# Moving a third query chunk's attention forward, parking its sums in DRAM, and cutting the last chunk and the K/V projections into halves

## The chip, the core and the metric

The kernel runs on one core of one Trainium2 chip. The metric is the device time of one execution in microseconds (us), as the median of several executions. Most executions of one kernel agree within 0.3%. Where two kernels are compared, the ratio is the mean time of one kernel's fast runs over that of the other's of the same rounds, so it is not quite the ratio of the medians quoted beside it. Chips and sessions differ a little (the kernel before took 2823 us in one session and 2825 to 2830 in the others), so experiments are compared by their ratio to the kernel before, measured on the same chip in the same call. A point is 1% of the time of the kernel before.

## The reference

Two kinds of layer alternate, A B A B, on `x` of shape 1 x 2048 x 1024, with 32 heads of 32:

```python
def A(x, wqkv, w_phi, wo):            # linear attention with feature maps
    q, k, v = split(x @ wqkv)
    pq, pk = q @ w_phi, k @ w_phi                       # per head, 32 x 32
    phi = lambda p: concat(softmax(p), softmax(-p))     # over 32 features
    kv = phi(pk).T @ v;  z = phi(pk).sum(rows)
    return (phi(pq) @ kv / (phi(pq) @ z + 1e-6)) @ wo
def B(x, wqkv, wo):                   # softmax attention
    q, k, v = split(x @ wqkv)
    return softmax(q @ k.T * 32**-0.5) @ v @ wo
x = x + A(layernorm(x)); x = x + B(layernorm(x))
x = x + A(layernorm(x)); x = x + B(layernorm(x))
```

The kernel has two passes of the same shape. I call them layer 1 and layer 2; each is the query side of an A layer followed by a B layer. Layer 1 also computes, after its B attention, the key side of the next A layer. That extra work makes the end of layer 1 heavier than the end of layer 2.

## The kernel before

The sequence is cut into four chunks of 512 rows (C), each of four key tiles of 128. A *step* of attention handles two key tiles, 256 queries (a half) and four heads (a head group; there are 8). It makes 8 score matmuls, two exps on ScalarE of 128 x 1024, and 16 matmuls into one accumulator `ND` in PSUM, whose left half is the numerator and whose right half is the denominator:

```python
    LAYOUT = {"wide": (0, 8), "mid": (2, 3), "narrow": (3, 1)}   # score tiles, background PSUM slots
    ...
    def step(self, q, kv, g, half, kc, begin, end, ...):   # 8 matmuls, then 2 exps
    def finish(self):                                      # one step later: 16 matmuls into ND
        ...
        if not end:
            return
        num, den = nd[:, 0:QH], nd[:, QH:C]
        if not last:                       # this query will see more keys later
            a = acc[0][g // 2][:, g % 2, half, :]          # numerator stays in SBUF
            if half == 0:
                self.dt = T("dt", [P, 2, QH], F32)         # ONE buffer
            ...
            DVE.tensor_tensor(out=a, in0=num, in1=a, op=ALU.add)
            DVE.tensor_tensor(out=dt[:, half, :], in0=den, in1=dn[:, half, :], op=ALU.add)
            if half == 1:                                  # denominator goes to DRAM
                for j in range(4):
                    SP.dma_start(out=den_d[acc[1]][g:g + 1, j, :, :], in_=dt[32 * j:32 * j + 1, :, :])
            return
        ...                                # else: add, reciprocal, multiply into oT
```

All other work (projections, layer norms, output projections) is *background*: Python generators, pumped between steps. A credit per step (`per`, in units of 512 columns of TensorE work) sets how much. `bg.until(name)` runs the rest of a generator with no attention between: a *flush*.

```python
            bg = Background(); set_mode("mid")
            bg.add("b0", b_proj(0, (1,)))
            bg.add("b1", rest1())                     # chunk 1: rest of A, K, V, Q
            attend(att, att.block(qs[0], 0, 4, ...), bg, 10)
            bg.until("b1")                            # flush
            set_mode("narrow")
            bg.add("b2", to_b(2)); bg.add("b3", to_b(3))
            attend(att, att.block(qs[0], 4, 8, ...), bg, 5)
            attend(att, att.block(qs[1], 0, 8, ...), bg, 5)
            bg.until("b2")
            attend(att, att.block(qs[0], 8, 12, ...), bg, 6)
            attend(att, att.block(qs[1], 8, 12, ...), bg, 6)
            bg.until("b3")                            # flush
            for i in range(NCH):
                ...                                   # after(i-1): output projection, and in layer 1
                                                      # the next A layer's key side ("follow-up")
                block = (att.block(qs[i], 0, 16, ...) if i > 1
                         else att.block(qs[i], 12, 16, ...))
                attend(att, block, bg, 3.5)
            settle(att); bg.until("after2")
            set_mode("wide")
            drain(after(3, oT[-1], layer, True))      # the tail: no attention left
```

PE, ScalarE, VectorE and Pool instructions keep the order in which this Python code emits them.

The softmax here doesn't subtract the row's maximum and nothing guards it: scores larger than these inputs give would overflow.

Of the kernel before, what the change touches and what calls it, by code (L numbers as in the profile page):

```python
# [32 lines left out]
def kernel(  # L33
# [14 lines left out]
    def ppf(w):  # L48
# [7 lines left out]
        w=3, c8=3, x=2, q=2, kv=2, st=2, E=6, ea=8, acc=4, f=5, r=3, nd=2,  # L56
# [29 lines left out]
    den_d = [Dr(f"den_d{i}", [G, 4, 2, QH], F32) for i in range(2)]  # L86
# [87 lines left out]
    def mm8(ps, lhsT, rhs):  # L174
        for po in range(G):
            mm(ps, lhsT(po), rhs(po), po == 0, po == G - 1)
            if po == 3:
                yield 4, False
# [3 lines left out]
    def ln_gen(x, res, fast=False):  # L182
        ps = ps512()
        yield from mm8(ps, lambda po: ones_bf[:], lambda po: x[:, po, :])
        m = T("f", [P, C], F32)
        DVE.tensor_scalar(out=m[:], in0=ps, scalar1=1.0 / D, scalar2=None, op0=ALU.mult)
        yield 4, True
        xc = T("c8", [P, G, C], BF16)
        res["xc"] = xc
        sqs = []  # L190

        def centre(po):
            DVE.tensor_tensor(out=xc[:, po, :], in0=x[:, po, :], in1=m[:], op=ALU.subtract)  # L193

        ps = ps512()
        for po in range(G):
            centre(po)
            if po % 4 == 0:
                sq4 = T("st", [P, 4, C], BF16)
            sq = sq4[:, po % 4, :]  # L200
            if fast:
                SC.activation(out=sq, in_=xc[:, po, :], func=ACT.Square)
            else:
                DVE.tensor_tensor(  # L204
                    out=sq, in0=xc[:, po, :], in1=xc[:, po, :], op=ALU.mult
                )
            sqs.append(sq)
        yield from wait(3)
        for po in range(G):
            mm(ps, ones_bf[:], sqs[po], po == 0, po == G - 1)  # L210
            if po < G - 1 and po % 2:
                yield 2, False
        lnv = T("f", [P, C], F32)
        rstd = T("r", [P, C], F32)
        SC.activation(out=lnv[:], in_=ps, func=ACT.Ln, scale=1.0 / D, bias=eps_t[:])
        SC.activation(out=rstd[:], in_=lnv[:], func=ACT.Exp, scale=-0.5)
        yield 2, True

        diag = T("f", [P, 4, P], F32)
        rcol = T("rcol", [P, 4], F32)  # L220
        DVE.tensor_tensor(
            out=diag[:], in0=rstd[:].rearrange("p (t q) -> p t q", q=P),
            in1=ident[:].unsqueeze(1).to_broadcast([P, 4, P]), op=ALU.mult,
        )
        DVE.reduce_sum(out=rcol[:], in_=diag[:], axis=AX.X)
        if fast:
            ncol = T("nc", [P, 4], F32)
# [21 lines left out]
    def ak_gen(c, x, get, fast=False, res=None, hook=None):  # L249
        if c == 0:  # L250
# [6 lines left out]
        SP.dma_start(out=xa_d[c][:], in_=xc[:])  # L257
        SP.dma_start(out=ra_d[c][:], in_=rstd[:])
        va = []
        for i in range(2):  # L260
            v = T(f"acc{2 + 2 * (c % 2) + i}", [P, 2, G, P + 1], BF16)
            POOL.memset(v[:, :, :, P:P + 1], 1.0)
            va.append(v)
        for fc in range(2):
            w = get()
            for t in range(4):
# [12 lines left out]
        for fc in range(2):  # L279
            w = get()  # L280
            es = []
            for t in range(4):
# [33 lines left out]
            def kv_part(fc=fc, es=es):  # L316
                for gi in range(4):
                    g = fc * 4 + gi
                    ps = ps512()
                    for t in range(4):  # L320
                        for s in range(2):
# [4 lines left out]
                                t == 0 and s == 0, t == 3,  # L326
                            )
                    if c == 0:
# [6 lines left out]
                    yield 2.5, True  # L335
# [114 lines left out]
    def aq_gen(c, x, slabs, res, pause=6):  # L450
# [9 lines left out]
    def aq_finish(c, x, slabs, res):  # L460
        yield from proj_out(x, res["oT"], slabs)
        yield from ln_gen(x, res, PS["ns"] == 0)
        SP.dma_start(out=x_d[c][:], in_=x[:])

    def proj_out(x, oT, slabs):
        for ft in range(G):
            if ft % 4 == 0:
                w = slabs.get()
            ps = ps512()
# [4 lines left out]
            yield 4, True  # L474


    def bkv_gen(c, res, slabs, h, q=None):
# [24 lines left out]
        if q is not None:  # L502
            yield from bq_gen(q, xc, rstd, slabs, range(4 * h, 4 * h + 4))
# [13 lines left out]
    class Attention:  # L517
# [4 lines left out]
        def load(self, k0, k1, g, acc, first):  # L522
# [7 lines left out]
            if first:  # L530
                return kt, None
            dn = T("dn", [P, 2, QH], F32)
            for j in range(4):
                SP.dma_start(  # L534
                    out=dn[32 * j:32 * j + 32, :, :],
                    in_=den_d[acc[1]][g:g + 1, j, :, :].to_broadcast([DH, 2, QH]),
                )
            return kt, dn

        def block(self, q, k0, k1, acc, oT, first, last, before=None):  # L540

            kv = self.load(k0, k1, 0, acc, first)
            for g in range(G):
                if before and g in before:
                    before[g]()
                    kv = self.load(k0, k1, g, acc, first)
                nxt = None
                for half in range(2):
                    for kc in range(0, k1 - k0, 2):
                        self.step(q, kv, g, half, kc, kc == 0, kc + 2 == k1 - k0,  # L550
                                  acc, oT, first, last)
                        if nxt is None and g + 1 < G and not (before and g + 1 in before):
                            nxt = self.load(k0, k1, g + 1, acc, first)
# [3 lines left out]
        def step(self, q, kv, g, half, kc, begin, end, acc, oT, first, last):  # L557
# [23 lines left out]
            self.lag.append((kv, dn, g, half, kc, begin, end, acc, oT, first, last, es))  # L581

        def finish(self):

            kv, dn, g, half, kc, begin, end, acc, oT, first, last, es = self.lag.pop(0)
# [18 lines left out]
            if not last:  # L604
                a = acc[0][g // 2][:, g % 2, half, :]
                if half == 0:
                    self.dt = T("dt", [P, 2, QH], F32)
                dt = self.dt
                if first:
# [7 lines left out]
                if half == 1:  # L617
                    for j in range(4):
                        SP.dma_start(
                            out=den_d[acc[1]][g:g + 1, j, :, :], in_=dt[32 * j:32 * j + 1, :, :]  # L620
                        )
                return
            ndc = T("nd", [P, C], F32)
            if first:
                DVE.tensor_copy(out=ndc[:], in_=nd[:])  # L625
            else:
                DVE.tensor_tensor(
                    out=ndc[:, 0:QH], in0=num, in1=acc[0][g // 2][:, g % 2, half, :], op=ALU.add
                )
                DVE.tensor_tensor(out=ndc[:, QH:C], in0=den, in1=dn[:, half, :], op=ALU.add)  # L630
            rc = T("rc", [P, QH], F32)
            DVE.reciprocal(out=rc[:], in_=ndc[:, QH:C])  # L632
            DVE.tensor_tensor(
                out=oT[:, g, half * QH:(half + 1) * QH], in0=ndc[:, 0:QH], in1=rc[:],
# [75 lines left out]
    def run():  # L710
# [19 lines left out]
        drain(ln_gen(xs[0], res, True))  # L730
        for c in range(NCH):
# [12 lines left out]
            main = ak_gen(c, xs[c], iter(av + pk).__next__, True, res, hook)  # L744
            if c + 1 < NCH:
                xs[c + 1] = load_first(c + 1)
                drain(merge(main, ln_gen(xs[c + 1], nres, True), 4))
# [5 lines left out]
        def after(c, oT, layer, fast=False):  # L753
            x = load_x(c)
            sl = Slabs(["bo"] + (["av", "pk"] if layer == 0 else []))
            sl.prefetch()
            yield from proj_out(x, oT, sl)
            if layer == 0:
                yield from ak_gen(c, x, sl.get, fast)
                SP.dma_start(out=x_d[c][:], in_=x[:])  # L760
            else:
                yield from store_out(c, x)
# [8 lines left out]
        for layer in range(2):  # L771
# [4 lines left out]
            BKVQ = ["bk0", "bv0", "bq0", "bk1", "bv1", "bq1"]  # L776

            def to_b(c):
                x = load_x(c)
                res = saved[c] = {}  # L780
                sl = res["sl"] = Slabs(["pq", "ao"] + BKV)
                yield from aq_gen(c, x, sl, res)
                yield from b_proj(c, (0, 1))
                SP.dma_start(out=xb_d[c][:], in_=res["xc"][:])
                SP.dma_start(out=rb_d[c][:], in_=res["rstd"][:])

            def b_proj(c, parts):
                res = saved[c]
                for h in parts:
                    yield from bkv_gen(c, res, res["sl"], h, qs.get(c))  # L790
# [5 lines left out]
            r0["sl"] = Slabs(["ao"] + BKVQ)  # L796
            r1["sl"] = Slabs(["ao"] + BKVQ)
# [5 lines left out]
            early = [T(f"acc{4 + k}", [P, 2, 2, C], BF16) for k in range(4)]  # L803
            es1 = [early[g // 2][:, g % 2] for g in range(G)]
# [12 lines left out]
            drain(b_proj(0, (0,)))  # L817

            def rest1():
# [3 lines left out]
                yield from b_proj(1, (0, 1))  # L823

            bg = Background()
            set_mode("mid")
            bg.add("b0", b_proj(0, (1,)))
            bg.add("b1", rest1())
            acc = [([T(f"acc{k}", [P, 2, 2, QH], F32) for k in range(4)], 0), None]
            attend(  # L830
                att,
                att.block(qs[0], 0, 4, acc[0], None, True, False, {4: lambda: bg.until("b0")}),
                bg, 10,
            )
            settle(att)
            bg.until("b1")
            acc[1] = ([T(f"acc{4 + k}", [P, 2, 2, QH], F32) for k in range(4)], 1)
            set_mode("narrow")
            bg.add("b2", to_b(2))
            bg.add("b3", to_b(3))  # L840
            attend(att, att.block(qs[0], 4, 8, acc[0], None, False, False), bg, 5)
            attend(att, att.block(qs[1], 0, 8, acc[1], None, True, False), bg, 5)
            bg.until("b2")
            attend(att, att.block(qs[0], 8, 12, acc[0], None, False, False), bg, 6)
            attend(att, att.block(qs[1], 8, 12, acc[1], None, False, False), bg, 6)
            bg.until("b3")
            oT = [None] * NCH
            for i in range(NCH):
                if 0 < i < NCH - 1:
                    qs[i + 1] = T("q", [P, G, C], BF16)  # L850
                    bg.add(f"q{i + 1}", next_q(i + 1, qs[i + 1]))
                if i:
                    bg.add(f"after{i - 1}", chain(wait(3), after(i - 1, oT[i - 1], layer)))
                bg.until(f"q{i}")
                oT[i] = T("c8", [P, G, C], BF16)
                block = (
                    att.block(qs[i], 0, S // P, None, oT[i], True, True) if i > 1
                    else att.block(qs[i], 12, 16, acc[i], oT[i], False, True)
                )
                attend(att, block, bg, 3.5)  # L860
            settle(att)
            bg.until(f"after{NCH - 2}")
            set_mode("wide")
            drain(after(NCH - 1, oT[-1], layer, True))
# [99 lines left out]
    def store_out(c, x):  # L964
        for t in range(4):
# [42 lines left out]
```

## Time and profile before

Median 2822.97 us of three runs (2821.79 to 2825.78). The top of the profile's page gives busy time and share of the span:

```profile
span 2830.9 us, 89391 instructions
PE 2375.8 (84%) x40048; PEld 1151.2 (41%) x40048; DVE 1326.5 (47%) x2205; ACT 2156.5 (76%) x2489; POOL 95.7 (3%) x87
```

No engine is the limit throughout, so the page's shares say little and the stages say more. Where ScalarE is saturated, an exp starts every 0.91 us (median), so a step costs 1.83 us and the 512 steps of a layer cost about 935 us at the least. The table gives busy time by stretch (from:to, length, then busy time of PE, weight loads, VectorE, ScalarE and Pool with counts, granted clock, DMA share and GB/s). The rows are: all of layer 1 from its first exp to layer 2's first; all of layer 2 to the end; the two flushes of layer 1; the third and the fourth query's attention in layer 1; layer 1's tail; layer 2's tail.

```profile
282.60:1658.10 1375.50, 1152.15 (x20740) 561.38 (x20736) 664.74 (x1030) 1054.96 (x1206) 47.66 (x40) 0.93 0.35 111
1658.10:2830.90 1172.80, 975.22 (x17848) 466.50 (x17843) 472.83 (x819) 970.60 (x1062) 0.00 (x0) 0.95 0.30 97
369.60:412.50 42.90, 42.10 (x796) 20.06 (x792) 17.83 (x26) 0.04 (x1) 0.00 (x0) 1.00 0.62 189
786.60:805.10 18.50, 13.57 (x240) 6.58 (x236) 4.73 (x7) 0.03 (x2) 0.00 (x0) 1.00 0.47 148
941.40:1229.00 287.60, 240.46 (x5024) 124.57 (x5023) 134.07 (x185) 254.02 (x289) 19.18 (x15) 0.95 0.32 104
1229.00:1495.50 266.50, 216.56 (x4322) 107.25 (x4315) 104.16 (x138) 247.87 (x279) 16.45 (x15) 0.96 0.21 70
1495.50:1658.10 162.60, 143.87 (x730) 63.85 (x733) 97.34 (x153) 53.52 (x90) 11.69 (x8) 0.92 0.41 136
2803.50:2830.90 27.40, 21.33 (x110) 10.12 (x109) 12.73 (x43) 0.00 (x0) 0.00 (x0) 0.81 0.10 39
```

Read ScalarE's column against the length. In the flushes it is 0.04 of 42.9 and 0.03 of 18.5: TensorE projects and nobody does exps. In the third query's attention it is 254 of 288; the rest is lost to waits.

From the list of waits (engine, tile and line <- what it waited for: total us, times, longest us), the lines about denominators. `dt` is the tile that is stored to DRAM (`den_d`), `dn` the one loaded back; in later lists `S` is a score tile, `E` its exps and `BG` a background tile in PSUM:

```profile
PE ND L594 <- DVE dt L614: 98.8, 48, 10.2
DVE dt L614 <- DMA den_d<-dt: 44.7, 30, 3.8
DVE nd L630 <- DMA dn<-den_d: 25.1, 22, 4.9
DVE dt L614 <- DMA dn<-den_d: 11.7, 7, 2.2
```

VectorE waits for the store of the last `dt` before it may write the next, then TensorE waits for VectorE to release `ND`. Part of the first line is another thing: the serial VectorE chain of `aq_scale`, ten short instructions and a 3.34 us reciprocal, holds `ND` for up to 10.2 us, twice a layer.

### The profile page before, as it was taken

How to read it: one execution, taken by the hardware profiler on the slowest of the kernel's cores; microseconds unless marked ns; L12 is line 12 of the kernel's file. 1: busy time of each engine (PE TensorE's matmuls, PEld its weight loads, DVE VectorE, ACT ScalarE, POOL GpSimd, SP SyncE). 2: the span in 40 equal slices, each digit the busy share in tenths (PEclk: the TensorE clock that was granted, in tenths of full speed). 3: DMA queues.
4: the chain of work that ended last, by engine and by line, in shares of the span. 5: the costliest groups of instructions: out<-in, count | busy, mean ns of one | idle time of the engine just before them, and what ended most of it. 6: DMA issues, size and time to landing. Idle time of an engine off the chain costs nothing. (4 is left out here: it accounts for less than half of the span.)

```text
span 2830.9 us, 89391 instructions
## 1 busy us (share of the span) xinstructions
PE 2375.8 (84%) x40048; PEld 1151.2 (41%) x40048; DVE 1326.5 (47%) x2205; ACT 2156.5 (76%) x2489; POOL 95.7 (3%) x87
## 2 busy tenths in 40 slices
PE   7988997996778879888778899799777778988877
PEld 4543443442333444444334344344333334434333
DVE  5776544425457653454524745444443773323213
ACT  5543728997668889898894354699874889999996
POOL 1320000000000010010101000000000000000000
PEclk9999998998998999999999999999888899999999
DMA  8424363342443422323105154425234242221110
GB/s 241 127 88 137 122 192 98 136 136 64 151 130 89 150 96 84 125 77 125 62 17 175 45 187 140 140 70 188 85 103 159 83 125 91 92 76 47 52 41 16
DMA packets 231392, 308.48 MB, mean 109 GB/s; under 512 B 36640, under 2 KB 194336, under 8 KB 223840
## 3 DMA queue, kind: packets, MB, share of 16 engines
q1 hardware_dynamic: 230192, 301.20, 33.5%
q8 instruction: 313, 5.13, 0.7%
q10 hardware_dynamic: 816, 1.57, 0.2%
q14 instruction: 71, 0.58, 0.1%
HBM read 239.14 MB, written 58.33 MB: 105 GB/s over the span
## 5 line engine op out<-in xcount | busy, mean ns | idle before, releaser
L576 ACT ACTIVATE E<-S 128x1024 bf16<-128x1024 f32 x2048 | 1911.8, 1149 | 369.4 <-PE S L567 368.5
L594 PE MATMUL ND<-E,kv 128*32 128x256 bf16 x8192 | 652.5, 286 | 246.5 <-DVE dt L614 98.8
L567 PE MATMUL S<-q,kv 32*128 32x256 bf16 x8192 | 570.2, 283 | 79.5 <-ACT E L576 43.0
L594 PE MATMUL ND<-E,ones 128*32 128x256 bf16 x8192 | 589.6, 286 | 0.0
L169 PE MATMUL BG<-c,w 128*32 128x512 bf16 x7680 | 482.1, 385 | 33.4 <-DVE x L473 14.7
L594 PEld LDWEIGHTS <-kv 128*32 128x32 bf16 x8192 | 278.7, 99 | 496.0 <-issue 311.5
L567 PEld LDWEIGHTS <-kv 32*128 32x128 bf16 x8192 | 177.3, 93 | 406.1 <-issue 403.5
L594 PEld LDWEIGHTS <-ones 128*32 128x32 bf16 x8192 | 271.7, 100 | 54.1 <-issue 5.2
L169 PEld LDWEIGHTS <-w 128*32 128x32 bf16 x7680 | 191.4, 97 | 240.1 <-issue 107.2
L632 DVE RECIPROCAL rc<-nd 128x256 f32<-128x256 f32 x128 | 224.4, 1753 | 4.4
L169 PE MATMUL BG<-w,c 128*32 128x512 bf16 x3328 | 212.9, 388 | 12.1 <-DVE st L239 5.1
L473 DVE TENSOR_TENSOR x<-BG,x 128x512 bf16<-128x512 f32 x128 | 87.1, 689 | 193.7 <-PE BG L169 175.4
L625 DVE COPY nd<-ND 128x512 f32<-128x512 f32 x64 | 44.1, 689 | 260.9 <-PE ND L594 260.6
L165 PE MATMUL BG<-c,w 128*128 128x512 bf16 x640 | 150.6, 396 | 1.6 <-DVE nd L625 1.6
L169 PEld LDWEIGHTS <-c 128*32 128x32 bf16 x3328 | 83.8, 97 | 105.3 <-issue 46.8
L306 POOL TENSOR_TENSOR ea<-ea,sm 128x512 bf16<-128x512 bf16 x64 | 93.4, 1459 | 776.8 <-ACT E L576 328.1
L165 PEld LDWEIGHTS <-c 128*128 128x128 bf16 x704 | 69.3, 99 | 86.3 <-issue 6.6
L165 PE MATMUL BG<-w,c 128*128 128x512 bf16 x448 | 99.4, 383 | 2.0 <-ACT st L924 2.0
L300 DVE TENSOR_REDUCE sm<-ea 128x32 f32<-128x1024 bf16 x64 | 77.8, 1215 | 48.2 <-ACT ea L296 35.0
L165 PEld LDWEIGHTS <-w 128*128 128x128 bf16 x640 | 64.5, 101 | 85.3 <-issue 17.5
L387 DVE TENSOR_TENSOR f<-BG,r 128x512 f32<-128x512 f32 x64 | 43.3, 689 | 106.6 <-PE BG L169 76.7
L486 DVE TENSOR_TENSOR st<-BG,r 128x512 bf16<-128x512 f32 x64 | 44.2, 691 | 97.7 <-PE BG L169 93.3
(110 smaller groups left out, 1584.6 us busy)
## 6 DMA issues: line engine op xcount, KB each, us to landing
w<-in_B_wqkv_dram SPq DMA_DIRECT2D x48, 1024.0 KB
dn<-den_d SPq DMA_DIRECT2D x320, 64.0 KB
x_d<-x SPq DMA_DIRECT2D x16, 1024.0 KB
x<-x_d SPq DMA_DIRECT2D x16, 1024.0 KB
w<-in_A_wo_dram SPq DMA_DIRECT2D x16, 1024.0 KB
w<-in_B_wo_dram SPq DMA_DIRECT2D x16, 1024.0 KB
kv<-kT_d SPq DMA_DIRECT2D x32, 512.0 KB
kv<-v_d SPq DMA_DIRECT2D x32, 512.0 KB
```

The costliest lines, as they stand in the source:

```text
L165: PE.matmul(ps, lhsT=lhsT, rhs=rhs, start=start, stop=stop, skip_group_check=True)
L169: PE.matmul(ps[cols, :], lhsT=lhsT[:, cols], rhs=rhs, start=start, stop=stop, tile_position=(0, 32 * j), skip_group_check=True,)
L300: DVE.reduce_sum(out=ss[:], in_=e[:].rearrange("p s (h f) -> p s h f", f=DH), axis=AX.X)
L306: (POOL if s else DVE).tensor_tensor(out=e[:, s, :].rearrange("p (h f) -> p h f", f=DH), in0=e[:, s, :].rearrange("p (h f) -> p h f", f=DH ...
L387: DVE.tensor_tensor(out=pq[:], in0=ps, in1=rstd[:], op=ALU.mult)
L473: DVE.tensor_tensor(out=x[:, ft, :], in0=ps, in1=x[:, ft, :], op=ALU.add)
L486: DVE.tensor_tensor(out=st[:, gi, :], in0=ps, in1=rstd[:], op=ALU.mult)
L567: PE.matmul(tiles[j // 2][:, o:o + QH], lhsT=kv[rows, 0, (kc + k) * P:(kc + k + 1) * P], rhs=q[rows, g, half * QH:(half + 1) * QH], start= ...
L576: SC.activation(out=e[:], in_=tiles[i][:].rearrange("p (j k q) -> p j k q", k=2, q=QH), func=ACT.Exp, scale=SCALE,)
L594: PE.matmul(nd[rows, part * QH:(part + 1) * QH], lhsT=ones_bf[:, 0:32] if part else kv[:, 1, col:col + 32], rhs=es[j // 2][:, j % 2, i, :] ...
L625: DVE.tensor_copy(out=ndc[:], in_=nd[:])
L632: DVE.reciprocal(out=rc[:], in_=ndc[:, QH:C])
```

## The change

Its intent is to give ScalarE exps earlier and to leave TensorE less work without them. It has these parts:

- **Early third query.** Chunk 2's queries attend to the first 12 key tiles (96 steps) before the last keys exist. Their sums, and those of the second query, are parked in DRAM (`nd_d`).
- **Halves.** The last query chunk attends in two halves of 256, so that the first half's follow-up can run behind the second half's attention.
- **Half heads.** K and V of chunks 1 to 3 are made in two background pieces; a block waits for the second only at its fifth head group.
- **Denominators.** Four row stores and four broadcast loads a head group become one 256 KB transfer each, and the buffers go from one to three (store) and two (load).
- **Pauses and rates.** `pause` 6 to 8 and layer-norm wait 3 to 5 (pumps skipped so that a producer can finish); credit 6 to 5 in two blocks and 3.5 to 4.5 at the end.

```diff
-        w=3, c8=3, x=2, q=2, kv=2, st=2, E=6, ea=8, acc=4, f=5, r=3, nd=2,
+        w=3, c8=3, x=2, q=3, kv=2, st=2, E=6, ea=8, acc=4, f=5, r=3, nd=3, pn=2,
 ...
-            dn = T("dn", [P, 2, QH], F32)
-            for j in range(4):
-                SP.dma_start(out=dn[32 * j:32 * j + 32, :, :],
-                    in_=den_d[acc[1]][g:g + 1, j, :, :].to_broadcast([DH, 2, QH]))
+            if isinstance(src, tuple):
+                dn = T("pn", [P, 2, QH], F32)
+                SP.dma_start(out=dn[:], in_=den_d[src[1]][:, g, :, :])
 ...
+                DVE.tensor_tensor(out=ndc[:], in0=nd[:], in1=dn[:], op=ALU.add)
+            if isinstance(dst, int):
+                SP.dma_start(out=nd_d[dst][:, g, half, :], in_=ndc[:])
+                return
 ...
-            bg.add("b2", to_b(2))
-            bg.add("b3", to_b(3))
-            attend(att, att.block(qs[0], 4, 8, acc[0], None, False, False), bg, 5)
-            attend(att, att.block(qs[1], 0, 8, acc[1], None, True, False), bg, 5)
-            bg.until("b2")
-            attend(att, att.block(qs[0], 8, 12, acc[0], None, False, False), bg, 6)
-            attend(att, att.block(qs[1], 8, 12, acc[1], None, False, False), bg, 6)
-            bg.until("b3")
+            bg.add("b1b", b_proj(1, 1)); bg.add("q1", b_query(1))
+            bg.add("b2a", to_b(2)); bg.add("b2b", rest_b(2))
+            bg.add("b3a", to_b(3)); bg.add("b3b", rest_b(3))
+            attend(att, att.block(qs[0], 4, 8, (acc, 0), (acc, 1), need("b1b")), bg, 5)
+            bg.until("q1")
+            attend(att, att.block(qs[1], 0, 8, None, 0), bg, 5)
+            bg.until("b2a")
+            attend(att, att.block(qs[0], 8, 12, (acc, 1), (acc, 0), need("b2b")), bg, 5)
+            attend(att, att.block(qs[1], 8, 12, 0, 1), bg, 5)
+            attend(att, att.block(qs[2], 0, 12, None, 2), bg, 5)
+            bg.until("b3a")
 ...
+                    for half in range(2):
+                        if half:
+                            bg.add("after3", chain(wait(3), after(3, oT[3], layer, n=QH)))
+                        block = att.block(qs[i], 0, S // P, None, oT[i], halves=(half,))
+                        attend(att, block, bg, 4.5)
```

(Lines are joined here and there; the plumbing of a chunk length `n` through the layer norm, projections and key side is left out.)

## The prediction

> **What bounds it now.** The busy table gives ScalarE 2156 us of 2831 and TensorE 2376; neither binds throughout. Attention's exps take 0.90 us start to start, a floor of 927 us a layer. (The Trainium skill, "ScalarE: Activation LUTs", What ACT_TABLE_LOAD costs, gives 186 + 0.833 N ns less 93 of overlap, 0.95 us at N = 1024; the trace is a little better.) Yet first to last exp takes 1213 us in layer 1 and 1145 in layer 2 (timeline). The lost time:
>
> - flushes, projections on TensorE with no attention between: 43 us (the list of waits: ACT E on PE S, longest 42.9) and 18.5 us, each once a layer;
> - tails: 163 us after layer 1's attention, 27 after layer 2's;
> - attention steps (1.83 us when ScalarE-bound) of 2.5 to 2.9 us where VectorE's chains hold up the one ND accumulator: the a/b chain (10 us, one 3.34 us reciprocal in it), layer norms, key softmax;
> - DRAM round trips of denominators: "DVE dt waits for den_d" 44.7 us, "DVE nd waits for dn" 25.1 us; dn loads are 2.2% of the chain of waits.
>
> **What the change does.** Arithmetic is nearly unchanged. By the order of instructions, TensorE work left without attention (at 0.216 us per 512 columns) goes, per layer, from 41.5 + 13.0 us to 13.8 + 11.2 + 11.2 (layer 1 also 6.0). Layer 1's tail goes only from 126 to 120, layer 2's from 15.6 to 7.8.
>
> Estimates from the trace: the first flush drops from 43 to 15 us (-28). The 18.5 us flush becomes two of 17.5 (2.7 us a tile with one background PSUM slot, as in the old flush): +16. Four small loads and stores of den become one each of 256 KB, and the stored buffer goes from one to three: -10 to -20 a layer. New nd_d loads are issued only some two steps before use: +4 in each of three blocks (the skill, "DMA: Bandwidth & Descriptors", Anatomy of one DMA: about 2 us fixed; dn waits here were 2 to 3.5). Longer pauses before layer-norm and a/b consumers, and blocks that evict ND rarely: -5 to -10.
>
> Layer 1's end gains little: the first half of the last chunk's follow-up is unfinished when attention ends, so about 19 us of its matmuls drain in the narrow mode (40 us with waits), then the second half repeats a layer norm (42): 82 us where the old tail spent 68. And in the third query's last block VectorE needs an estimated 2.3 us a step, above ScalarE's 1.83. So layer 1: 0 to -15. Layer 2: about -35, the output tail -11 of it.
>
> **Prediction: 2778 us**, 80% range 2720 to 2830. Chances: faster by over 2% 0.36, within 2% 0.60, slower 0.04.
>
> **What would show it.** Right: the 43 us ScalarE gap shrinks to 15; two new gaps of 15 to 20 us, at the end of the second query's first block and in the middle of the first query's third; "dt waits for den_d" vanishes; layer 1's third-query last block runs at 2.4 us a step or more; layer 1's last exp to layer 2's first does not shrink; last exp to end shrinks to 16. ScalarE's busy time stays near 2156. Wrong: long VectorE waits for nd_d loads; denominators still waited for.
>
> **What would make it wrong.** If the denominator and ND stalls are worth the full 35 us a layer and the 12-tile block runs at 1.83 us, it lands near 2720. If nd_d loads queue behind 1 MB weight loads, every half-block stalls and the gain is gone.

## The result, and the profile after

Median 2855.53 us of four runs (2853.92 to 2858.19), against 2822.99 for the kernel before: ratio 1.0115, 95% interval 1.0097 to 1.0132. The change makes the kernel slower by 1.15%. The top of the page after:

```profile
span 2854.6 us, 90880 instructions
PE 2373.1 (83%) x40925; PEld 1173.2 (41%) x40960; DVE 1354.5 (47%) x2192; ACT 2154.1 (75%) x2487; POOL 95.6 (3%) x87
```

The arithmetic is the same, as predicted. Busy time by stretch, after. The rows: layer 1; layer 2; the three flushes of layer 1; the early block of the third query, and its last 54 us by themselves; the third query's last block with the flush that follows it, and that flush by itself; the fourth query's attention; layer 1's tail; layer 2's tail.

```profile
282.80:1699.10 1416.30, 1160.92 (x21386) 576.93 (x21392) 684.22 (x1041) 1051.45 (x1205) 47.36 (x38) 0.94 0.41 136
1699.10:2854.60 1155.50, 965.03 (x18104) 472.78 (x18096) 481.29 (x795) 971.68 (x1062) 0.00 (x0) 0.95 0.40 129
370.20:387.00 16.80, 14.22 (x284) 7.00 (x280) 6.53 (x10) 0.02 (x1) 0.00 (x0) 1.00 0.45 141
604.00:620.40 16.40, 11.41 (x196) 5.33 (x192) 4.39 (x6) 0.04 (x2) 0.00 (x0) 1.00 0.40 123
660.80:676.90 16.10, 11.35 (x196) 5.29 (x192) 4.15 (x6) 0.00 (x0) 0.00 (x0) 1.00 0.30 94
782.30:975.90 193.60, 163.34 (x3074) 79.48 (x3074) 36.58 (x57) 178.24 (x194) 0.00 (x0) 0.96 0.35 117
921.50:975.90 54.40, 43.16 (x720) 19.34 (x720) 3.46 (x5) 54.40 (x60) 0.00 (x0) 1.00 0.14 45
1110.50:1221.70 111.20, 77.59 (x1528) 39.71 (x1524) 78.80 (x98) 69.55 (x82) 11.88 (x10) 0.88 0.37 120
1212.70:1221.70 9.00, 6.16 (x112) 3.00 (x115) 2.93 (x6) 0.00 (x1) 0.00 (x0) 1.00 0.19 61
1221.70:1513.80 292.10, 244.85 (x5498) 133.02 (x5491) 146.07 (x207) 257.36 (x292) 23.68 (x19) 0.96 0.37 126
1513.80:1699.10 185.30, 143.73 (x1120) 68.20 (x1133) 107.93 (x188) 48.85 (x89) 11.80 (x9) 0.89 0.45 148
2838.90:2854.60 15.70, 9.58 (x94) 7.84 (x93) 8.37 (x27) 0.00 (x0) 0.00 (x0) 1.00 0.09 34
```

Layer 1 lost 40.8 us (1375.5 to 1416.3) and layer 2 gained 17.3 (1172.8 to 1155.5). (The two make 23.5, not the 32.5 between the medians, because the profiled run of the kernel before took 2832.7 us, 10 above its median.) By the rows, layer 1's loss is third query +17, fourth query +26 and tail +23, less 12 in the flushes and 13 in the first two queries' blocks. The predicted gaps are where they were predicted: 16.8 in place of 42.9, and two of 16 in place of one of 18.5. Three rows carry the loss:

- The row from 921.5 is the kernel at its most efficient and its most wasteful: ScalarE is busy for 54.4 of 54.4 us, and TensorE makes 720 matmuls, which are 30 steps' own 24 matmuls each. No background at all runs behind them.
- The third query's last block then takes 102 us from its first exp to its last for 32 steps, 3.2 us a step, and a flush of 9.0 us follows. VectorE is busy for 78.8 us of the 111.2.
- The tail of layer 1 is 185 us where it was 163.

The list of waits has hardly a line left for the denominators' stores and loads (4.0 us of a layer norm's tile and 0.2 of a weight load, where the kernel before had over 80), and none for the parked sums (`nd_d`). New in it are TensorE's waits for keys (`kT_d`) and values (`v_d`):

```profile
PEld L567 <- DMA kv<-kT_d: 21.3, 11, 4.7
PE S L567 <- DMA kv<-kT_d: 17.9, 9, 4.2
PEld L599 <- DMA kv<-v_d: 17.9, 4, 6.3
PE ND L599 <- DMA kv<-v_d: 16.0, 4, 5.8
```

TensorE's matmuls wait 33.9 us in total for loads of K and V (second and fourth line; the weight-load lines are the same waits seen by the other queue). In the kernel before, the only such line is 0.2 us, of a weight load; with the denominators' change alone (`old_den_rows`, below) the matmuls wait 5.5 us for K.

So I had two questions: why did the end of layer 1 get worse, and what did each part of the change do?

### The profile page after: what moved, and what is told of

The parts are those of the page before. It is cut to its first block, busy times and chain, and to the rows that moved or that the text cites. A ratio compares the mean times of both kernels' runs of the same rounds, so it can differ in the third digit from the quotient of the medians.

```text
span 2854.6 us, 90880 instructions
## 1 busy us (share of the span) xinstructions
PE 2373.1 (83%) x40925; PEld 1173.2 (41%) x40960; DVE 1354.5 (47%) x2192; ACT 2154.1 (75%) x2487; POOL 95.6 (3%) x87
## 5 line engine op out<-in xcount | busy, mean ns | idle before, releaser
L567 PE MATMUL S<-q,kv 32*128 32x256 bf16 x8192 | 561.6, 281 | 90.6 <-ACT E L576 33.5
L170 PE MATMUL BG<-c,w 128*32 128x512 bf16 (+1 forms) x8192 | 506.8, 381 | 43.7 <-DVE q L515 23.9
L170 PEld LDWEIGHTS <-w 128*32 128x32 bf16 x8192 | 210.8, 97 | 255.9 <-issue 130.4
L170 PE MATMUL BG<-w,c 128*32 128x512 bf16 x3584 | 232.2, 392 | 42.3 <-DVE f L238 20.3
L477 DVE TENSOR_TENSOR x<-BG,x 128x512 bf16<-128x512 f32 (+1 forms) x144 | 89.7, 631 | 214.5 <-PE BG L170 204.8
L627 DVE COPY nd<-ND 128x512 f32<-128x512 f32 x96 | 66.0, 688 | 234.8 <-PE ND L599 234.0
L170 PEld LDWEIGHTS <-c 128*32 128x32 bf16 x3584 | 94.0, 97 | 143.6 <-issue 82.4
L166 PE MATMUL BG<-c,w 128*128 128x512 bf16 (+1 forms) x624 | 133.5, 371 | 4.0 <-DVE c L641 1.3
L515 DVE TENSOR_TENSOR q<-BG,r 128x512 bf16<-128x512 f32 x64 | 44.2, 691 | 108.4 <-PE BG L170 86.3
L438 DVE TENSOR_TENSOR ea<-BG,ea 128x512 bf16<-128x512 f32 x96 | 64.2, 689 | 61.6 <-PE BG L170 61.5
```

Of the source, the lines that this page charges most:

```text
L166: PE.matmul(ps, lhsT=lhsT, rhs=rhs, start=start, stop=stop, skip_group_check=True)
L170: PE.matmul(ps[cols, :], lhsT=lhsT[:, cols], rhs=rhs, start=start, stop=stop, tile_position=(0, 32 * j), skip_group_check=True,)
L438: DVE.tensor_tensor(out=es[g][:, s, :], in0=ps, in1=es[g][:, s, :], op=ALU.mult)
L477: DVE.tensor_tensor(out=x[:, ft, :], in0=ps, in1=x[:, ft, :], op=ALU.add)
L567: PE.matmul(tiles[j // 2][:, o:o + QH], lhsT=kv[rows, 0, (kc + k) * P:(kc + k + 1) * P], rhs=q[rows, g, half * QH:(half + 1) * QH], start= ...
L627: DVE.tensor_copy(out=ndc[:], in_=nd[:])
```

## The experiments

Theories. **COVER**: attention steps are what projections hide behind; the early block uses 96 of them where little is left to hide, and takes them from the end of layer 1, where three follow-ups must hide. **HALVES**: cutting the last chunk costs by itself. **DVE**: short last blocks bring a reciprocal every second step and collide with the follow-up's VectorE work. **PARK**: DRAM traffic of the parked sums. Later: **SPLIT** and **ROUNDTRIP** for the half heads.

### First call: undo parts, or do one alone

**`whole_last_l1`**: the changed kernel, last chunk whole in layer 1.

```diff
+                elif layer == 0:
+                    attend(att, att.block(qs[i], 0, S // P, None, oT[i]), bg, 4.5)
                 else:
                     for half in range(2):
 ...
-            bg.until("after3")
+            bg.until("after3" if layer else "after2")
             # layer 0: drain(after(NCH - 1, oT[-1], layer, True))
```

> The changed kernel, with layer 1's last query chunk whole again (halves kept in layer 2). Theory HALVES (splitting the last chunk in layer 1 costs time, because about 19 us of matmul work of the first half's follow-up drains in the narrow PSUM layout after attention has ended, and the second half repeats a layer norm): the stretch from layer 1's last exp to layer 2's first falls from 185 us to about 163, and the second half of the attention of that chunk loses its follow-up work as well (145 to about 125); total about 2855 - 35 = 2820 us. Rival COVER alone (the loss comes from the third query's 96 early steps, which take attention away from the end of layer 1): the tail falls but the follow-ups of chunks 0 to 2 stay as slow as they were, so at most -15, about 2840 us.

Measured: 2837.11 us, ratio 1.0038 [1.0016, 1.0059], so 0.8% faster than the change. The tail went from 185 to 163 us as expected, but the second half's attention stayed at 143 us (145 before the edit), not 125. The result lies close to COVER's "about 2840". But the edit does give back the tail's 22 us, so in this kernel the halves cost what they add to the tail.

**`early_half`**: the changed kernel, only 4 of 8 head groups early.

```diff
-            attend(att, att.block(qs[2], 0, 12, None, 2), bg, 5)
+            attend(att, att.block(qs[2], 0, 12, None, 2, gs=range(4)), bg, 5)
 ...
+                    if i == 2:
+                        block = chain(
+                            att.block(qs[i], 12, 16, 2, oT[i], gs=range(4)),
+                            att.block(qs[i], 0, S // P, None, oT[i], gs=range(4, G)),
+                        )
```

> The changed kernel, with only 4 of the 8 head groups of the third query attended early (48 steps, not 96); the other 4 attend late to all 16 key tiles at once. Theory COVER (58 of the 96 early steps have no projection to hide, while at the end of layer 1 three follow-ups must hide behind 192 steps where the kernel before had 288): the early block falls from 194 to about 100 us, the work left to drain after layer 1's attention falls, and the third query's late block runs at about 2.4 us a step instead of 3.2; total -30 to -45, about 2818 us, three quarters of it in layer 1. Rival HALVES: no change beyond -10. Rival PARK (the DRAM traffic of parked sums is what costs): a quarter of that traffic goes, so at most -10.

Measured: 2808.08 us, ratio 0.9941 [0.9926, 0.9956], 1.7% faster than the change. The early block is 105 us, layer 1's tail is 136 us although the halves are kept, and the third query's late work takes 199 us for 80 steps, 2.5 a step. COVER's numbers came out, the total (some 48 us) a little above its 30 to 45; HALVES and PARK, which allowed 10 us, did not. Layer 1 gained 41 us of it (1416.3 to 1375.3) and layer 2 only 6, though both layers had the same steps moved back.

**`both`**: the two edits together.

> Both edits of the two runs before: 4 of 8 head groups early, and layer 1's last chunk whole. If COVER and HALVES are separate costs they add up to about -70: 2785 us, faster than the kernel before (2823). If they are one cost seen twice (the narrow drain disappears with either edit), about 2810 us.

Measured: 2814.89 us, ratio 0.9965 [0.9949, 0.9981]. It is no better than `early_half` alone, in fact 0.2% worse. So the halves are no separate cost: with enough cover they help, without it they hurt. HALVES falls as a theory of its own.

**`old_den_rows`**: the kernel *before*, with only the denominators' change.

```diff
-        rc=2, kvm=2, ...
+        rc=2, dn=2, dt=2, kvm=2, ...
-            for j in range(4):
-                SP.dma_start(out=dn[32 * j:32 * j + 32, :, :], in_=den_d[...]...to_broadcast(...))
+            SP.dma_start(out=dn[:], in_=den_d[acc[1]][:, g, :, :])
-                    for j in range(4):
-                        SP.dma_start(out=den_d[acc[1]][g:g + 1, j, :, :], in_=dt[32 * j:32 * j + 1, :, :])
+                    SP.dma_start(out=den_d[acc[2]][:, g, :, :], in_=dt[:])
```

> The kernel BEFORE with only the denominators' change: one 128-row store and one 128-row load of 256 KB a head group in place of four stores of one row and four broadcast loads, and two buffers for each. My prediction took 10 to 20 us a layer for this: about 2793 us. If the waits for denominators in the list were hidden behind the three score tiles, nothing: 2823 us.

Measured: 2772.36 us, ratio 0.9816 [0.9801, 0.9831]. This was the surprise: one small part of the change is worth 53 us by itself. The rest of the change therefore costs some 83 us, not 32.

### Second call: each other part alone, on top of that

The base of these four is the denominators' change; the second query's sums are parked in DRAM as in the change. I did not run that base by itself. It differs from `old_den_rows` by the parking, by a third store buffer, by the place of the second query's projection (after all its K and V) and by where some tiles lie. The traces show no cost of it: from a layer's first exp to the third query's first it takes 634.3 and 633.2 us in the two layers of `old_den_rows` and 631.5 and 631.6 in those of `den_halves`; from there to the layer's end 719.0 and 502.6, and 718.9 and 503.5 in `den_split`, whose late part is the base's.

**`den_early`**: plus the early block of 96 steps (and the third query's projection moved ahead of it).

```diff
+            attend(att, att.block(qs[2], 0, 12, None, 2), bg, 5)
             bg.until("b3a")
```

> The kernel before with the denominators' change (2772 us in the run just seen; first query's sums in SBUF, second query's parked in DRAM as in the changed kernel) plus ONLY the third query's early block of 96 steps: no half heads of K and V, no halves of the last chunk, old pauses. Theory COVER: the early block has 78 of 96 steps with nothing to hide, and layer 1's follow-ups no longer fit: 15 us of matmul work flushed in the narrow layout before the last chunk, 132 (was 126) left for the tail, the third query's last block at 3 us a step; about 2772 + 55 = 2827 us. Rival (the early block is harmless, the loss lies in the half heads and the halves): 2765 to 2780 us.

Measured: 2819.49 us, ratio 0.9963 [0.9946, 0.9979], that is +1.5 points on the base. COVER named +55 us, and about +42 came. The third query's last block in layer 1 takes 92 us up to its last exp and a flush of 28 us follows it. Against `old_den_rows`, layer 1 is 41 us longer (1353.2 to 1394.3) and layer 2 only 4 (1135.8 to 1139.8).

**`den_split`**: plus the half heads.

```diff
             bg.add("b1b", b_proj(1, 1)); bg.add("q1", b_query(1))
             bg.add("b2a", to_b(2)); bg.add("b2b", rest_b(2)); bg.add("b3a", to_b(3)); bg.add("b3b", rest_b(3))
             # and need("b1b"), need("b2b"), need("b3b") at the fifth head group of a block
```

> The same base (2772) plus ONLY the half heads: K and V of chunks 1 to 3 in two background pieces, with the waits in the middle of a block. The first flush falls by 26 us a layer, but narrow flushes of 7.8 and 17.3 us of matmul work (old: one of 13.0) and a store-to-load round trip of K and V of some 6 us in the middle of blocks come back: expected within 10 us of 2772. Theory COVER says this part is near neutral; rival SPLIT says it costs most of the 83 us that lie between 2772 and 2855: 2830 us or more.

Measured: 2825.7 us, ratio 0.9981 [0.9964, 0.9999], +1.65 points. My "within 10 us" missed: the half heads cost some 47 us. The trace shows where. From the timeline around a block that needs the new values (start, length, engine, instruction, and in brackets the idle time before it and what ended it):

```profile
807.35 0.36 SPq L505 DMA_DIRECT2D v_d<-st  x1
...
815.64 0.80 SPq L528 DMA_DIRECT2D kv<-v_d  x2
...
817.79 0.40 PE L599 MATMUL ND<-E,kv 128*32 128x256 bf16 x4 [5.36 <-DMA kv<-v_d]
...
819.42 1.94 ACT L576 ACTIVATE E<-S 128x1024 bf16<-128x1024 f32 x2 [6.86 <-PE S L567]
```

The values' store is issued at 807.35, the load that reads them only at 815.64, and the first matmul with them starts at 817.79: 10.4 us from store to use. ScalarE stands idle for the 6.9 us before 819.42. The Trainium skill, "DMA: Bandwidth & Descriptors", Two DMAs through the same engine are not ordered, says that a DMA which reads what an earlier one wrote must wait for the first one's completion semaphore; this trace agrees: the store landed at 815.58, just before the load was issued. Its 8.2 us are not unusual (16 such stores of this run took 4.5 to 9.2 us, median 7.6), and a 1 MB weight load, issued 0.8 us before it, landed only at 813.11. How much of the 8.2 us is queueing behind such loads was not varied. Over the whole kernel:

```profile
PE ND L599 <- DMA kv<-v_d: 38.8, 9, 7.1
PE S L567 <- DMA kv<-kT_d: 15.3, 7, 4.1
```

That is 54 us of waits for a loss of 47, some 6 of them in the base too (5.5 in `old_den_rows`). The kernel before made K and V long before they were used and had none of these waits.

**`den_halves`**: plus the halves, in both layers.

```diff
-                    attend(att, att.block(qs[i], 0, S // P, None, oT[i]), bg, 3.5)
+                    for half in range(2):
+                        if half:
+                            bg.add("after3", chain(wait(3), after(3, oT[3], layer, n=QH)))
+                        attend(att, att.block(qs[i], 0, S // P, None, oT[i], halves=(half,)), bg, 3.5)
```

> The same base (2772) plus ONLY the last chunk in two halves, in both layers. Theory COVER: here the last chunk has 63 free steps, so the first half's follow-up hides completely: tail matmul work 126 to 101 in layer 1, paid for by slower steps in the second half; layer 2's tail falls from 25 to 16; total 2755 to 2768 us. Rival HALVES (halving costs by itself): 2785 us or more.

Measured: 2749.18 us, ratio 0.9711 [0.9696, 0.9725], -1.05 points, better than expected. Layer 1's tail is 135 us in place of 165. The same edit that lengthened the tail in the change shortens it here, because the steps to hide the first half's follow-up are there.

**`den_waits`**: plus the longer pauses.

```diff
-        yield from wait(3)
+        yield from wait(3 if fast else 5)
-    def aq_gen(c, x, slabs, res, pause=6):
+    def aq_gen(c, x, slabs, res, pause=8):
```

> The same base (2772) plus ONLY the longer pauses (8 for 6 before the query features' output, 5 for 3 in the layer norm). My prediction took 5 to 10 us a layer off for these: 2757. Against it: the pauses push projections back, so the narrow flush before the last key chunk grows from 13.0 to 23.3 us of matmul work, at 1.4 us each: +14 a layer, 2800 us.

Measured: 2797.92 us, ratio 0.9886 [0.9870, 0.9902], +0.7 points, as the counter-argument said. The flush before the last key chunk grows from 18.5 to 34.9 us. A pause is paid for in the pumps that it leaves empty.

### Third call: why the denominators matter, additivity, VectorE

**`den_layout_only`** and **`den_buffers_only`** take the denominators' change apart, on the kernel before.

```diff
 # den_layout_only: one 128-row transfer each way, separate DRAM tensors; dt and dn keep 1 buffer
 # den_buffers_only: the eight small transfers as before, and
-        rc=2, kvm=2, ...
+        rc=2, dn=2, dt=2, kvm=2, ...
```

> The kernel before with the denominators moved as 128 rows in one transfer (four row stores and four broadcast loads become one each), and read and written in separate DRAM tensors, but still ONE buffer each for dt and dn. Both edits together gave -1.8%. If the number of transfers and their issue on the queue is the cost: -1.5% or more. If what costs is that one buffer's store or load must land before the next may start: at most -0.5%.

> The kernel before with two buffers each for dt and dn, the eight small transfers a head group left as they are. If buffers are the cost: -1.3% or more, and the waits of VectorE's dt for the store of den_d vanish. If the number and kind of transfers is: at most -0.5%.

Measured: layout only 2812.5 us, 0.9942 [0.9919, 0.9966]; buffers only 2770.84 us, 0.9795 [0.9773, 0.9816]. A second buffer for two tiles of 2 KB a partition is the gain; the number of transfers is worth little, and nothing more once the buffers are there (0.9816 for both). With one buffer and the new layout VectorE still waits 61.6 us for stores of `den_d`. After the buffers the list of waits has this line for the accumulator, against 98.8 before, and none of VectorE for `den_d` or `dn`:

```profile
PE ND L594 <- DVE dt L614: 52.8, 14, 10.1
```

What is left has a longest wait of 10.1 us: the `aq_scale` chain. The skill, "Perfetto Trace Analysis", Identifying Performance Opportunities, Optimization Strategy, names this reading for the engine that should be saturated: the same gap repeating "can mean there isn't enough SBUF/PSUM for the next tile to be allocated". Here the gaps were VectorE's, 30 waits of up to 3.8 us, which then held up TensorE, and the second buffer removed them.

**`changed_unsplit`**: the changed kernel without the half heads and with the old pauses (rates 5, 5, 6, 6, 4.5).

> The changed kernel without the half heads of K and V and with the old pauses; early third query, halves of the last chunk, single denominator transfers all kept. The parts measured one by one on top of the denominators' change: half heads +1.65% of the time before, pauses +0.70%. If the parts add, 1.0115 - 0.0235 = 0.988, about 2791 us. If the half heads only cost where the third query attends late (they were meant to work with it), it stays above 1.000.

Measured: 2827.25 us, ratio 0.9993 [0.9974, 1.0012]. The edit gains 1.2 points, half of the 2.35 that the parts cost one by one. The parts do not simply add. In the changed kernel the half heads and the pauses push work into the early block, which has room for it: 770 background matmuls run there, and 354 without them. Alone, either part lengthened the flush before the last key chunk (38.1 us in `den_split`, 34.9 in `den_waits`, for 18.5); in the change that flush is gone. The end of layer 1, from the second query's last exp on, stays as it was (588 us, and 586 without them).

**`no_recip`**: the changed kernel with the last reciprocal replaced by a constant scale. Wrong result.

```diff
-            DVE.reciprocal(out=rc[:], in_=ndc[:, QH:C])
-            DVE.tensor_tensor(out=dst[...], in0=ndc[:, 0:QH], in1=rc[:], op=ALU.mult)
+            DVE.tensor_scalar(out=dst[...], in0=ndc[:, 0:QH], scalar1=1.0 / S, scalar2=None, op0=ALU.mult)
```

> The changed kernel with the reciprocal of the attention's ends removed and the sum scaled by a constant in its place: WRONG RESULT on purpose; 1.75 us of VectorE work an end goes, nothing else. Theory DVE (in layer 1 the third query's last block, 3.2 us a step, is held up by VectorE, where an end with a reciprocal every second step meets the follow-up's layer norm and key softmax): that block falls from 111 to 85 us or less, its counterpart in layer 2 by less than 10; total -25 to -45 us. Rival (the volume of background matmuls or the granted clock sets that block): it stays above 105 us, total above -15.

Measured: 2802.31 us, ratio 0.9901 [0.9880, 0.9921], 2.1 points better than the change, more than expected in total. The third query's last block in layer 1 fell only from 111 to 95 us, between the two theories:

```profile
1105.80:1200.60 94.80, 72.63 (x1525) 38.01 (x1520) 49.24 (x80) 68.58 (x81) 11.87 (x10) 0.93 0.44 140
```

Both figures include the flush after the block (9.0 us, and 7.3 here). ScalarE's own work is 69.6 us before the edit and 68.6 after it. So of the 42 us that this stretch loses (111.2 less 69.6), the reciprocals account for 16 and 26 remain: 7 in the flush, and 19 in the block with waits that no run takes apart. Its counterpart in layer 2 fell from 77 to 63, more than the 10 I allowed. DVE is shown to be a part, not the whole.

### Fourth call: the dose of the early block, and the round trip

**`halves_early2`, `halves_early4`, `halves_early8`**: `den_halves` with 2, 4 or 8 head groups of the third query early (and, in all three, its projection moved ahead).

```diff
+            attend(att, att.block(qs[2], 0, 12, None, 2, gs=range(K)), bg, 5)    # K = 2, 4, 8
 # late: block(qs[2], 12, 16, ...) for the first K groups, block(qs[2], 0, 16, ...) for the others
```

> Best kernel so far (denominator buffers plus halves, 0.971 of before) with the third query attended early for 2 of 8 head groups: 24 steps, of which only 6 have nothing to hide, since 19 us of projections are left at that point. Theory COVER: the harm of the early block is the steps it spends with nothing to hide, so this dose does no harm: it replaces the 18.5 us flush before the last key chunk and leaves layer 1's tail at 101 us of matmul work; 0.962 to 0.971. Rival (early attention costs in proportion to its steps, by parked sums, extra loads and short blocks): a quarter of the +1.5% that 96 steps cost, 0.974 or more.

> The same with 4 of 8 head groups: 48 steps, 30 of them with nothing to hide; in layer 1 the first half's follow-up no longer ends in time (116 us of matmul work in the tail, against 101). Theory COVER: worse than 24 steps by 15 to 25 us, about 0.975. Rival (proportional): 0.978.

> The same with all 8 head groups: 96 steps, 78 with nothing to hide. Theory COVER: the loss grows faster than the dose, because in layer 1 each step taken from the end now leaves work in the narrow flush and the tail: 1.000 (the changed kernel without half heads gave 0.9993). Rival (proportional to steps): 0.986.

Measured, with `den_halves` as dose 0. "Idle steps" are the early steps with no background in the order of instructions; the tail runs from layer 1's last exp to layer 2's first; the last column gives the lengths of layer 1 and layer 2, by the profiled run:

| early steps | idle steps | median us | ratio to before | layer 1's tail, us | layers 1 and 2, us |
|---|---|---|---|---|---|
| 0 | 0 | 2749.18 | 0.9711 | 134.9 | 1337.8, 1128.3 |
| 24 | 6 | 2732.41 | 0.9662 [0.9642, 0.9682] | 136.1 | 1324.1, 1122.2 |
| 48 | 30 | 2767.17 | 0.9788 [0.9767, 0.9809] | 171.2 | 1358.3, 1124.8 |
| 96 | 78 | 2850.21 | 1.0080 [1.0062, 1.0098] | 221.1 | 1435.1, 1131.1 |

The two ends of the scale by stretch. First `halves_early2`: layer 1, layer 2, its early block, and layer 1's tail.

```profile
282.50:1606.60 1324.10, 1133.35 (x21396) 570.20 (x21392) 675.96 (x1029) 1048.36 (x1205) 47.37 (x38) 0.95 0.43 140
1606.60:2728.80 1122.20, 964.47 (x18104) 475.47 (x18096) 473.15 (x783) 968.79 (x1062) 0.00 (x0) 0.96 0.39 127
778.90:826.80 47.90, 44.94 (x930) 23.26 (x930) 10.60 (x15) 44.76 (x48) 0.00 (x0) 1.00 0.57 186
1470.50:1606.60 136.10, 118.11 (x618) 55.21 (x621) 83.46 (x141) 43.37 (x80) 5.85 (x4) 0.91 0.45 146
```

Then `halves_early8`: layer 1, layer 2, its early block, the flush before the fourth query, and layer 1's tail.

```profile
282.90:1718.00 1435.10, 1185.13 (x21396) 583.20 (x21392) 684.30 (x1041) 1049.18 (x1204) 47.33 (x38) 0.94 0.41 134
1718.00:2849.10 1131.10, 967.63 (x18104) 474.64 (x18096) 480.95 (x795) 969.52 (x1062) 0.00 (x0) 0.96 0.40 132
779.60:960.70 181.10, 149.00 (x2658) 69.97 (x2658) 18.91 (x27) 176.37 (x192) 0.00 (x0) 1.00 0.29 94
1190.20:1218.70 28.50, 20.64 (x363) 10.52 (x356) 8.37 (x13) 0.04 (x1) 0.00 (x0) 0.83 0.13 41
1496.90:1718.00 221.10, 166.70 (x1578) 82.44 (x1581) 121.09 (x211) 52.12 (x94) 16.29 (x13) 0.86 0.41 134
```

Both early blocks are fast; both keep ScalarE nearly full. The difference is paid 400 to 900 us after the block begins: 28.5 us of flush and 85 us of tail. The effect changes its sign between 24 and 48 early steps, which a cost proportional to the early steps cannot do. This point alone is weak: from 24 to 96 steps the times rise almost in a straight line (1.5 to 1.7 us a step), and the step from 0 to 24 also moves the third query's projection. The two layers decide it. Both have the same early steps, the same short blocks and the same parked sums, but only layer 1 has the heavy follow-ups; from 24 to 96 steps layer 1 grows by 111 us and layer 2 by 9. So the loss is cover that is missing at layer 1's end, and not a cost of the early steps themselves. A dose of 24 steps gives the fastest kernel, 3.4% below the kernel before.

**`split_no_roundtrip`**: `den_split`, whose blocks load the first chunks' K and V in place of their own. Wrong result; sizes and counts of transfers are the same.

```diff
-            SP.dma_start(out=kt[:, 0, 0:n * P], in_=kT_d[:, g, k0 * P:k1 * P])
+            SP.dma_start(out=kt[:, 0, 0:n * P], in_=kT_d[:, g, 0:n * P])
-                in_=v_d[:, g, k0:k1, :],
+                in_=v_d[:, g, 0:n, :],
```

> The half-heads kernel (0.998 of before), whose attention blocks load the keys and values of the first chunks in place of their own: WRONG RESULT on purpose; the same number and size of transfers, but no load has to wait for a store that was made just before. Theory ROUNDTRIP (the half heads lose because K and V, stored in the middle of a block, are needed at once through DRAM: gaps of 3.8, 2.8, 6.3, 6.9 and 6.0 us a layer): about -40 us, 0.984. Rival (the narrow flushes and the denser background are the cost): at most -10 us, 0.995 or more.

Measured: 2770.65 us, ratio 0.9799 [0.9777, 0.9822], 1.8 points below `den_split` and level with the base. In its list of waits TensorE's matmuls have one line left for K and none for V:

```profile
PE S L567 <- DMA kv<-kT_d: 10.9, 8, 4.1
```

ROUNDTRIP holds. Without it the half heads would be about neutral; I had predicted a small gain for them and left the wait out. (All loads here read the first chunks, so the edit also changes which DRAM rows are read; that was not tested apart.)

## Why the prediction was wrong

I predicted 2778 us, and 2855.5 was measured. The kernels above form a chain from the kernel before to the change, each link one part:

| kernel | ratio to before | link |
|---|---|---|
| before | 1.0000 | |
| `old_den_rows` | 0.9816 | denominators: -1.8 |
| `den_halves` | 0.9711 | halves: -1.05 (and second query parked) |
| `halves_early8` | 1.0080 | early third query: +3.7 |
| `changed_unsplit` | 0.9993 | credit 3.5 to 4.5 at the end: -0.9 |
| the change | 1.0115 | half heads, pauses, credit 6 to 5: +1.2 |

A link's size depends on where it stands in the chain (the early block alone was +1.5, the halves turn from loss to gain), so the table is an order of building, not a sum of fixed prices. The links were measured in different calls, each ratio to about 0.2 points. The higher credit at the end helps by pumping more of the follow-up between steps: layer 1's tail falls from 221 to 175 us, the flush before the fourth query from 28.5 to 6.3, and the steps there get slower.

What held:

- **The flushes.** "43 to 15" was 42.9 to 16.8, and "two of 17.5" were 16.4 and 16.1.
- **The tails.** Layer 1's tail was said not to shrink; it grew from 163 to 185. Layer 2's fell from 27.4 to 15.7 (predicted 16).
- **Denominator waits** all but vanish, and ScalarE's busy time stayed (2154). The parked sums caused no waits, less than the +4 in each of three blocks that I had put in.
- **VectorE above ScalarE in the third query's last block**: "2.4 us a step or more" was 3.2.

What failed, step by step:

1. **"Layer 1: 0 to -15."** It lost 41 us. I counted the work left after attention (+14 us at the end; the tail grew by 23), put the third query's last block at 2.3 us a step (it took 3.2) and had no term for the fourth query's attention (266.5 to 292.1 us): the early block itself was priced as neutral. I had read from the order of instructions how much was drained at the end, but not that the 96 steps were taken from a place where each had been hiding something: 288 steps covered layer 1's follow-ups before, 192 do after. The dose experiment shows it: +3.7 points for 96 steps, -0.5 for 24, and the growth is in layer 1 alone. In the blocks that remain, the denser background met a reciprocal every second step (`no_recip`: 16 us in the third query's last block and its flush, 2.1 points in all).
2. **A term that was not in the sum**: the store-to-load round trip of half-made K and V. I took -28 and +16 a layer for the flushes of the half heads and nothing for the wait behind them. It is 33.9 us of matmul waits in the change (5.5 in `old_den_rows`, which has no half heads), and 1.8 points, some 51 us, in the pair `den_split` and `split_no_roundtrip` (an edit that also frees the loads at the starts of blocks from their stores).
3. **"Longer pauses ... -5 to -10"** had the wrong sign: +20 us alone (`den_waits`).
4. **"Four small loads and stores become one ... -10 to -20 a layer"** was too small, and did not tell its two causes apart. Alone it is -53 us for both layers, and it is the second buffer that brings it, not the number of transfers. Without this part the change would have looked worse still.
5. **"Layer 2: about -35"** was mis-sized: -17. The third query's last block (with a flush of 2 us) and the first half of the fourth took 77 and 127 us, where 32 and 64 steps at 1.83 would be 59 and 117, and 17.6 of the 33.9 us of waits for K and V fall in this layer.

Still open: what the remaining 19 us of the third query's last block are made of; why undoing half heads and pauses in the changed kernel gains only half of what they cost alone (the moved work explains the direction, no run isolates it, and that run also has credit 6 for 5); and the granted clock, which differs between these stretches (0.88 in the 111 us stretch, 0.96 in the one after it) and was not varied by itself.

## What to carry to other kernels

Where one engine's steps hide another engine's work, count those steps as a stock: before moving a block forward, list at each place how many steps have something to hide and how much must hide there later, and move only as many as have something to cover. A block that runs at full speed with nothing behind it is not a gain. Before restructuring, give a second buffer to any tile whose writer waits for its own last store, and make data that passes through DRAM well before it is needed.

## What the Trainium skill lacked or had wrong

- "ScalarE: Activation LUTs", What ACT_TABLE_LOAD costs: an estimate by its formula is 0.946 us for back-to-back exps of 1024 columns with immediate scale. These traces show 0.913 us start to start at the median of all 2048 in the kernel before, and 0.903 at the 25th per cent, a little under the page. The exps here read PSUM, and that section does not say for which memory its formula holds.
- "DMA: Bandwidth & Descriptors", Two DMAs through the same engine are not ordered: it gives the rule that a reader must wait for the writer's semaphore, but no price for a store followed by a dependent load. Here it was 10.4 us from the issue of a 512 KB store to the first matmul on the reloaded values, 8.2 of them until the store had landed, and some 51 us of the kernel's time over both layers.
- "Perfetto Trace Analysis", Optimization Strategy, advises interleaving regimes in which the most-contended engine differs. It does not say that what one regime can hide is a limited stock. Here 24 steps moved forward gave -0.5 points, 48 gave +0.8 and 96 gave +3.7.
